# A second table of rank offsets for a list scheduler, by kind of work and by stretch of its plan

## The chip, the cores and the metric

The kernel runs on one core of a Trainium2 chip. The metric is device time in microseconds (us) of one execution; several executions are timed and their median is taken. TensorE is called PE below (PEld is its weight load), VectorE DVE, ScalarE ACT, GpSimd POOL, and SyncE SP; SP issues every DMA of this kernel.

## The reference, cut to what matters

Two attention layers read the same input `x` (2048 tokens, width 640, 32 heads of 20), and a gate per token mixes their outputs. Layer A works through four segments of 512 tokens, with a causal softmax inside the segment and a linear memory that is carried from one segment to the next; layer B is attention in a sliding window of 256.

```python
# layer A, segment s of 4 (H = 32 heads, Dh = 20)
logits = einsum("bhqd,bhkd->bhqk", qs, ks) * scale + mask
a_dot = einsum("bhqk,bhkd->bhqd", softmax(logits), vs)
num = einsum("bhld,bhde->bhle", phi(qs), M)
den = einsum("bhld,bhd->bhl", phi(qs), z)[..., None] + 1e-6
o = g * num / den + (1 - g) * a_dot
M = M + einsum("bhld,bhle->bhde", phi(ks), vs)
z = z + einsum("bhld->bhd", phi(ks))
...
# layer B
scores = where((i >= j) & (i - j < 256), q @ k.T * Dh ** -0.5, -1e9)
b = (softmax(scores) @ v) @ wo
...
return gate * a + (1 - gate) * b        # gate = sigmoid((x * gate_w).sum(-1))
```

## The kernel before, in words

All work is cut into 16 groups T: four segments of 512 tokens times four sets of 16 heads (two sets for A, two for B). A group holds four units of four heads, which makes 64 units u. The work of a group:

- **Projections.** `gemm2` (line 548) makes 128 rows of q and k for 512 tokens, `v_mm` (line 689) 128 tokens of v. Operands are float32 split into a high and a low part in float32r, three products each (`PAIRS`). Both use half of the array at a time: rows 0 to 63 or rows 64 to 127. Two such matmuls on different halves run side by side, so what counts is how long each half is kept fed. The output projection uses `gemm2` too.
- **Weights.** Each weight tile is loaded by SP (`load`, line 494, tile `wst`), its high part is copied by ACT (`split_h`, line 486), its low part is made by POOL or DVE (`split_l`, line 502), and only then may a matmul use it. There are two staging buffers `wst` and three weight buffers `w`. The weights of v go the same way from `wvs` (line 519), five pieces each; tokens go from `xst` to `xhl`.
- **Maxima.** Stacked q and k of a unit come back from DRAM into `qks` (lines 762 to 767). `max_mm` (line 791) makes scores in a bank, DVE takes their row maximum (`max_red`, line 801, a reduction and a read of the accumulator), and the maxima go through DRAM (`dmx`, lines 817 and 821) to become two more rows of `qks`. Each half of the array has one bank for this (`NMX` is 1), so that the next matmul of maxima on that half waits for the reduction of the last.
- **Scores and values.** `st_mm` (line 845) makes the transposed scores, ACT takes their exponential (line 852), POOL cuts the masked corners (lines 858, 861), and `tiled_mm` (line 877) multiplies with v. It uses 32 columns of the array at a time, as do the reads and sums of the memory (lines 904 and 924). DVE, POOL and ACT then normalise, and SP stores the output (line 993).

**What sets the order.** `Plan.add` records each piece of work with an engine, an assumed duration, a due time and what it reads and writes. `Plan.order` is a list scheduler: it steps through a planned time, asks on each engine which recorded pieces could start, keeps those that could start within 3 ns (PE, `TP`) or 25 ns (the others, `TO`) of the earliest, and takes the one with the lowest rank. The rank is the due time plus an offset from the table `SHIFT`, by kind of work (18 kinds) and by 18 stretches of four units of due time. The order in which pieces are taken is the order in which each engine gets its instructions; engines then run in that order and wait on semaphores. Where a piece may go to two engines (a split to POOL or DVE, a copy to ACT or DVE), the scheduler chooses too. So an offset that swaps two pieces changes the planned time from there on, and with it every later choice.

Of the kernel before, what the change touches and what calls it, by code (L numbers as in the profile page):

```python
# [39 lines left out]
TP, TO, GP = 0.003, 0.0247, -0.9848  # L40
# [16 lines left out]
KINDS = dict(v_mm="v", max_mm="x", st_mm="s", tiled_mm="t", mem_add="a", split_h="h", split_l="l", m_high="e", m_low="e", v_out="e",  # L57
             y_out="e", phi_neg="p", phi_exp="p", phi_sum="p", max_red="r", st_exp="c", select="k", load="d", wv_load="d",
             qk_store="q", stack_read="z")
SHIFT = dict(  # L60
    a=(0.906, 0.762, 0.711, 0.288, -0.209, -3.157, -0.759, -0.444, 2.687, -1.073, -0.036, -1.619, 0.786, -0.987, 0.501, -1.076, 1.313, -0.983),
    c=(0.731, -0.093, -0.385, -0.167, -0.708, 0.703, 0.113, -0.061, 0.619, -0.11, -1.531, 0.072, -0.295, 0.055, -0.214, 0.043, -0.116, 0.411),
    d=(0.746, 0.239, 0.185, -0.082, 0.39, -0.063, 0.049, 0.317, -0.528, -0.276, -0.057, 0.559, -0.263, -1.344, -0.501, -0.266, 0.361, 1.353),
    e=(-4.249, 1.705, -0.128, 1.795, -1.311, 0.375, 0.842, -0.859, -0.461, 0.272, 0.494, -0.544, -0.178, -0.287, 2.233, 0.044, -2.89, 1.8),
# [12 lines left out]
    y=(-0.053, 0.457, 3.475, -0.742, 3.085, 0.939, 0.479, 0.047, 0.088, -0.236, -0.012, 0.322, 0.417, -0.102, -0.234, -0.183, 1.517, -0.737),  # L77
    z=(-1.272, 0.109, 0.692, -0.168, -1.3, -1.064, -0.08, -0.22, 0.395, -0.261, 1.106, -0.382, 1.384, 1.123, 1.476, -0.094, 0, -0.095))


def f(ap):
    return ap.bitcast(F32)
# [9 lines left out]
class Plan:  # L92
# [37 lines left out]
    def clock(self, t, dur, cols):  # L130
# [8 lines left out]
            left -= part  # L139
        return at - t  # L140

    def shift(self, z):

        name = z[4].__name__
        kind = ("y" if z[5][0][0] == "y" else "m") if name in ("gemm", "gemm2") else KINDS.get(name, "o")
        return SHIFT[kind][min(max(int((z[0] + 6) // 4), 0), 17)] if SHIFT else 0.0

    def link(self):
        items = [(*z[:19], z[19] + self.shift(z)) for z in sorted(self.items, key=lambda z: z[:2])]
# [79 lines left out]
    def order(self):  # L229
        items, deps, succ, miss, trail, uses, left, kind = self.link()  # L230
        n = len(items)
        ready = [0.0] * n
        free, cand, dma = {}, {}, [0.0] * self.RINGS
        for e in ENGINES:
            cand[e] = set()
            if e != "pe":
                free[e] = 0.0
        on = [None] * n

        def offer(i):  # L240
            for e in items[i][2].split("|"):
                cand[e].add(i)
        for i in range(n):
            if not miss[i]:
                offer(i)
        out, self.starts, self.ticks = [], [], {}
        last, port = ("half", 1.0), 0.0
        lane, turns = [0.0] * LANES, 0
        half = ("pe0", "pe1")
        avail, held, until, self.bank = {b: 0.0 for b in range(self.BANKS)}, {}, {}, {}  # L250
        while len(out) < n:
            best, front = None, None
            both = max(free["pe0"], free["pe1"])
            for e in ENGINES:
                pe = e[:2] == "pe"
                begin = both if e == "pe" else free[e]
                cold = pe and self.cold(begin)
                some = []
                for i in cand[e]:
                    at = begin  # L260
                    if pe:
                        at += max(0.0, self.LOAD[items[i][13][0]] - last[1])
                    z = max(at, ready[i]) + (items[i][15] if last[1] > 0.06 else 0.0)
                    if items[i][16] and e in ("dve", "pool"):
                        z = max(z, port)
                    if items[i][14]:
                        b = items[i][14]
                        if len(avail) < len(b) or any(held.get(k, 0) >= most for k, most, _ in b):
                            continue
                        if b[0][0] == "pj" and sum(held.get(k, 0) for k in ("st0", "st1", "pj")) >= CAP:  # L270
                            continue
                        z = max(z, sorted(avail.values())[len(b) - 1])
                    if "|" in items[i][2]:
                        ways = items[i][2].split("|")
                        z += FT * (items[i][0] > FL or items[i][0] < FE) * (items[i][3][ways.index(e)] - min(items[i][3])) + (DP if e == "dve" else 0.0)
                    if e == "sp":
                        z = max(z, lane[turns % LANES])
                    if items[i][10] and items[i][10][0] > BULK:
                        z = max(z, max(dma[:items[i][10][1]]) - BACK)
                    if e == "pe" and z <= both + 0.12 and (front is None or items[i][19] < front[1]):  # L280
                        front = z, items[i][19]
                    if e in half and front and front[1] < items[i][19] and z + items[i][3] > front[0] + GP:
                        continue
                    some.append((z, cold and items[i][12] < 900, items[i][19], i))
                if some:
                    most = min(some)[0] + (TP if pe else TO)
                    pick = min((z for z in some if z[0] <= most), key=lambda z: z[1:])
                    if best is None or pick < best[0]:
                        best = (pick, e)
            (start, _, _, i), e = best  # L290
            if "|" in items[i][2]:
                ways = items[i][2].split("|")
                start -= FT * (items[i][0] > FL or items[i][0] < FE) * (items[i][3][ways.index(e)] - min(items[i][3])) + (DP if e == "dve" else 0.0)
            elif e[:2] == "pe" and last[1] > 0.06:
                start -= items[i][15]
            for k, _, name in items[i][14]:
                held[k] = held.get(k, 0) + 1
                b = min(avail, key=lambda b: (max(avail[b], start - 1.0), avail[b]))
                self.bank[name] = b
                del avail[b]  # L300
            many = items[i][2].split("|")
            for z in many:
                cand[z].discard(i)
            on[i] = e
            out.append(i)
            dur, size = items[i][3], items[i][10]
            if len(many) > 1:
                dur = dur[many.index(e)]
            if e[:2] == "pe":
                start = max(start, (both if e == "pe" or last[0] != items[i][13][0] else free[e]) + self.turn(last, items[i][13]))  # L310
                dur = self.clock(start, dur, items[i][12])
                if e == "pe" or last[0] != items[i][13][0]:
                    free["pe0"] = free["pe1"] = start + (dur if e == "pe" else 0.0)
                last = items[i][13]
                if e != "pe":
                    free[e] = start + dur
                e = "pe"
            else:
                free[e] = start + dur
            self.starts.append(start)  # L320
            if items[i][16] and e in ("dve", "pool"):
                port = start + dur
            if size:
                took, rings, late = size
                done = 0.0
                for k in range(rings):
                    dma[k] = max(dma[k], start + dur + 1.2) + took
                    done = max(done, dma[k])
                done += DM + late
                lane[turns % LANES] = done  # L330
                turns += 1
            else:
                done = start + dur
            for name in uses[i]:
                left[name] -= 1
                until[name] = max(until.get(name, 0.0), done + (0.0 if e == "pe" else self.TO_PE))
                if not left[name]:
                    avail[self.bank[name]] = until[name]
                    held[kind[name]] -= 1
            for j in trail[i]:  # L340
                ready[j] = max(ready[j], start)
                miss[j] -= 1
                if not miss[j]:
                    offer(j)
            for j in succ[i]:
                to = "pe" if items[j][2][:2] == "pe" else items[j][2]
                lag = ((0.0 if e == "pe" else XS) if to == e and not size else self.TO_PE if to == "pe" else
                       0.0 if size else self.FROM_PE if e == "pe" else self.OTHER)
                ready[j] = max(ready[j], done + lag)
                miss[j] -= 1  # L350
                if not miss[j]:
                    offer(j)
        self.span = max(free.values())
        return [(items[i][4], items[i][5] + ((on[i],) if "|" in items[i][2] else ()), items[i][0]) for i in out]
# [934 lines left out]
```

## Time and profile before

| | |
|---|---|
| three runs | 992.94, 995.86 and 1002.88 us; median 995.86 |
| the profiled execution | 1005.22 us |
| its span, first to last instruction | 1003.5 us; 1.72 us lie around it |
| instructions in the span | 30570, of them 11295 matmuls |
| mean granted clock of PE | 0.989 of full |
| moved by DMA | 248.57 MB, 248 GB/s over the span |

A row of the list by time reads: start in us, duration in us, engine, line, operation, what it writes and reads, how many are merged (x), and in brackets how long the engine was idle before it and what ended that. In the list by window, each engine has its busy time in that window and, in brackets, the number of its instructions; behind it stand the granted clock, the busy share of the DMA engines, and GB/s. In the chain of waits, a row is start, duration and the work that stood last in the way. A matmul's duration in the trace reaches to its modelled end, and two matmuls overlap; the distance from start to start is what PE spends on one.

### The profile page before, as it was taken

Reading aid. Unit: us, or ns where it says so; the run is one execution under the profiler, and the core shown is the slowest. Engines: PE = TensorE matmul, PEld = TensorE weight load, DVE = VectorE, ACT = ScalarE, POOL = GpSimd, SP = SyncE. Lnnn points to the kernel's source line nnn. Section 1 sums busy time; section 2 is a strip of 40 time slices with the busy share of each in tenths; the row PEclk is TensorE's granted clock in tenths of the full one; section 3 lists DMA queues with packets and bytes.
Section 4 is the critical chain, followed back from the end, with each engine's and each line's share of the span. In section 5 each row is a group of like instructions: output and inputs, shape, how many; then the busy total and the mean of one; then the engine's idle time right before and its main releaser. Section 6 shows DMA issues by size and latency. Waiting matters only on the chain.

```text
span 1003.5 us, 30570 instructions
## 1 busy us (share of the span) xinstructions
PE 984.1 (98%) x11295; PEld 826.2 (82%) x11295; DVE 759.3 (76%) x2638; ACT 666.9 (66%) x1601; POOL 634.5 (63%) x862
## 2 busy tenths in 40 slices
PE   8999999999999899999999999899999999999998
PEld 6998888788788688888988898778888888987776
DVE  3269788888789586887867887569777886788944
ACT  4447767878578575776867676575677766765672
POOL 4335565847665587766966478576686657955660
PEclk8999999999999999999999999899999999999999
DMA  8898888789887889878798787859977898486532
GB/s 271 277 301 270 279 273 286 235 272 283 256 251 234 275 232 281 267 257 278 247 279 269 232 267 220 262 168 307 296 242 228 247 302 278 144 260 204 182 97 100
DMA packets 158037, 248.57 MB, mean 248 GB/s; under 512 B 52032, under 2 KB 68288, under 8 KB 157888
## 3 DMA queue, kind: packets, MB, share of 16 engines
q1 hardware_dynamic: 157888, 246.62, 78.0%
q8 instruction: 89, 1.46, 0.6%
q14 instruction: 60, 0.49, 0.1%
HBM read 150.88 MB, written 95.68 MB: 246 GB/s over the span
## 4 chain that ended last, share of the span: by engine, by line
PE 86%; DMA 6%; DVE 4%; SPq 1%; ACT 1%; POOL 1%; issue 1%; DVEq 0%
PE bank L548 40%; PE bank L689 14%; PE bank L877 14%; PE bank L791 8%; PE bank L845 7%; DMA wst<-wqk 3%; DVE bank L801 2%; PE bank L540 1%; PE bank L904 1%; DMA dphi<-phi 1%; DMA wvs<-wv 1%; DMA qks<-dkb 1%; DMA qks<-dmx 1%; PE bank L924 1%; POOL w L502 0%
## 5 line engine op out<-in xcount | busy, mean ns | idle before, releaser
L852 ACT ACTIVATE P<-bank 128x512 f32<-128x512 f32 (+2 forms) x768 | 382.2, 552 | 113.4 <-PE bank L845 73.2
L548 PE MATMUL bank<-xhl,w 64*128 64x512 f32 x2400 | 456.1, 402 | 0.5 <-DVE xhl L502 0.5
L548 PEld LDWEIGHTS bank<-xhl,w 64*128 64x128 f32 x2400 | 328.8, 188 | 12.0 <-DVE xhl L502 1.5
L791 PE MATMUL bank<-qks 60*128 60x384 f32 (+3 forms) x1024 | 302.7, 336 | 4.9 <-DMA qks<-dkb 4.1
L689 PE MATMUL bank<-wv,xhl 64*128 64x320 f32 (+1 forms) x1920 | 292.8, 318 | 2.2 <-ACT wv L486 1.9
L801 DVE CUSTOM_DVE_ANT_0 bank<-bank,mask_b 128x384 f32<-128x384 f32 (+2 forms) x512 | 259.3, 554 | 30.2 <-PE bank L791 24.2
L801 DVE CUSTOM_DVE_ANT_0 bank<-bank,mask_a 128x256 f32<-128x256 f32 (+3 forms) x512 | 239.5, 511 | 44.6 <-PE bank L791 29.3
L845 PE MATMUL bank<-qks 62*128 62x384 f32 (+3 forms) x1216 | 264.6, 303 | 5.3 <-ACT P L852 3.3
L689 PEld LDWEIGHTS bank<-wv,xhl 64*128 64x128 f32 x1920 | 248.9, 189 | 6.7 <-ACT wv L486 2.3
L548 PE MATMUL bank<-ohl,w 64*128 64x512 f32 x1050 | 225.4, 399 | 1.4 <-ACT P L852 1.0
L502 POOL TENSOR_TENSOR w<-wst,w 128x640 fp32r<-128x640 f32 x109 | 170.3, 1565 | 86.3 <-ACT w L486 81.0
L858 POOL TENSOR_SCALAR_AFFINE_SELECT P<-P 128x512 f32<-128x512 f32 x256 | 161.5, 638 | 89.1 <-ACT P L852 71.3
L845 PEld LDWEIGHTS bank<-qks 62*128 62x128 f32 x1216 | 197.5, 186 | 23.2 <-ACT P L852 5.3
L791 PEld LDWEIGHTS bank<-qks 60*128 60x128 f32 x1024 | 177.2, 185 | 23.7 <-issue 11.3
L877 PE MATMUL bank<-P,vau 128*32 128x384 f32 (+3 forms) x2432 | 160.3, 408 | 0.4 <-DVE mx L801 0.2
L548 PEld LDWEIGHTS bank<-ohl,w 64*128 64x128 f32 x1050 | 153.6, 186 | 7.8 <-ACT P L852 1.5
L801 DVE DVE_READ_ACCUMULATOR2_ANT mx<- 128x1 f32 x1024 | 143.2, 140 | 0.0
L877 PEld LDWEIGHTS bank<-P,vau 128*32 128x32 f32 x2432 | 69.5, 110 | 78.7 <-issue 63.2
L486 ACT ACTIVATE w<-wst 128x640 fp32r<-128x640 f32 x121 | 89.1, 738 | 39.8 <-DMA wst<-wqk 24.4
L948 DVE STREAM_TRANSPOSE ot<-bank 128x512 f32<-128x512 f32 x64 | 45.8, 715 | 71.1 <-PE bank L877 68.2
L861 POOL TENSOR_SCALAR_AFFINE_SELECT P<-P 128x512 f32<-128x512 f32 x112 | 71.3, 645 | 8.8 <-ACT P L852 7.7
L502 POOL TENSOR_TENSOR wv<-wvs,wv 128x322 fp32r<-128x322 f32 x80 | 66.3, 845 | 12.1 <-ACT wv L486 11.7
(74 smaller groups left out, 790.9 us busy)
## 6 DMA issues: line engine op xcount, KB each, us to landing
qks<-dqk SPq DMA_DIRECT2D x32, 1024.0 KB
wst<-wqk SPq DMA_DIRECT2D x80, 320.0 KB
qks<-dkb SPq DMA_DIRECT2D x24, 768.0 KB
qks<-dqb SPq DMA_DIRECT2D x32, 512.0 KB
o_dram<-ot SPq DMA_DIRECT2D x64, 256.0 KB
wst<-wo SPq DMA_DIRECT2D x41, 320.0 KB
wvs<-wv SPq DMA_DIRECT2D x16, 805.0 KB
xst<-o_dram SPq DMA_DIRECT2D x35, 256.0 KB
```

The lines of the kernel that those rows point to most:

```text
L486: nc.scalar.activation(dst, src, AF.Copy)
L502: EN[e].tensor_tensor(out=t[:, 1], in0=B.pop(src), in1=f(t[:, 0]), op=ALU.subtract)
L548: nc.tensor.matmul(B[key], B[wkey][64 * r:64 * r + 64, a, 128 * c:128 * c + 128], B[xkey, c][64 * r:64 * r + 64, b], start=start, stop=sto ...
L689: nc.tensor.matmul(B["v", T, b][:, :n], B[("x", s), c][64 * r:64 * r + 64, a, 128 * b:128 * b + 128], B["wv", T, c][64 * r:64 * r + 64, bb ...
L791: nc.tensor.matmul(psum(("mx", u, p, b, r))[:, :n], fr(q), keys(u, 3 * DH, r, p, c0, n), start=True, stop=True)
L801: nc.vector.tensor_tensor_reduce(out=x, in0=x, in1=mk, scale=1.0, scalar=BIG, op0=ALU.add, op1=ALU.max, accum_out=B["M", u][:, j:j + 1])
L845: nc.tensor.matmul(B[k][:, c:c + 128 * n], keys(u, K, r, p, WIN + 128 * kb, 128), fr(q[64 * r:64 * r + K, L * p + 128 * q0:L * p + 128 * ( ...
L852: nc.scalar.activation(B["P", u, b][:, 2 * r + p, c0:c1], B["st", u, b, p, r][:, c0:c1], AF.Exp, scale=SCALE)
L858: nc.gpsimd.affine_select(out=v, in_=v, pattern=[[0, 4], [1, 128]], compare_op=ALU.is_ge, fill=0.0, base=0, channel_multiplier=-1)
L861: nc.gpsimd.affine_select(out=v, in_=v, pattern=[[0, 4], [-1, 128]], compare_op=ALU.is_gt, fill=0.0, base=0, channel_multiplier=1)
L877: nc.tensor.matmul(o[32 * j:32 * j + 32, 128 * q0:128 * (q0 + n)], v[:, VA * h:VA * h + 32], t[:, j, c:c + 128 * n], start=(b == 0 and i = ...
L948: nc.vector.transpose(t, B["o", u])
```

## The change

A second table, `NUDGE`, holds 151 offsets by kind of work and by stretch of 12.5 us of planned time. At each step the scheduler works out which stretch the planned time of PE lies in, and the rank of each candidate gets the offset of its kind for that stretch, on top of the offset from `SHIFT`. Kinds and stretches that are not listed get nothing. The recorded pieces, their engines to choose from, sizes, buffers and assumed durations are as before.

```diff
+STEP = 12.5
+NUDGE = dict(
+    a={22: 0.6},
+    c={12: 1, 39: 1.4, 47: 1.4, 51: -1.1, 53: 2.1, 74: 2.9},
...
+    v={1: -2.021, 3: -0.77, 5: -0.05, 9: 0.113, 17: -1.1, 25: -0.007, 34: -0.164, 39: -0.3, 45: -0.23, 49: 0.034,
+       52: -0.858, 65: -0.3, 68: -0.04, 69: -0.61},
...
     def order(self):
         items, deps, succ, miss, trail, uses, left, kind = self.link()
         n = len(items)
+        nudge = [NUDGE.get(self.kind(z), {}) for z in items]
...
             both = max(free["pe0"], free["pe1"])
+            step = int(both / STEP)
...
                 for i in cand[e]:
+                    rank = items[i][19] + nudge[i].get(step, 0.0)
...
-                    if e == "pe" and z <= both + 0.12 and (front is None or items[i][19] < front[1]):
-                        front = z, items[i][19]
-                    if e in half and front and front[1] < items[i][19] and z + items[i][3] > front[0] + GP:
+                    if e == "pe" and z <= both + 0.12 and (front is None or rank < front[1]):
+                        front = z, rank
+                    if e in half and front and front[1] < rank and z + items[i][3] > front[0] + GP:
                         continue
-                    some.append((z, cold and items[i][12] < 900, items[i][19], i))
+                    some.append((z, cold and items[i][12] < 900, rank, i))
```

The lines named below stand 30 further down in the changed kernel (548 becomes 578, and so on). The order changes from the first microseconds to the end. Four places follow.

**SP at the start of the program, before the change.** `wst` are tiles of weights, `xst` of tokens, `wvs` the first weights of v, and `dqk0` gets its rows of padding.

```order
L494 DMA xst_160<-xt 128x512
L494 DMA wst_175<-wqk 128x640
L412 DMA bet_87<-beta 128x1x8
L519 DMA wvs_180<-wv 128x5x322
L494 DMA xst_195<-xt 128x512
L494 DMA wst_206<-wqk 128x640
L455 DMA dqk0_108<-ot_158 128x128 x4
```

SP at the same place, with the change:

```order
L524 DMA xst_160<-xt 128x512
L442 DMA bet_87<-beta 128x1x8
L524 DMA wst_176<-wqk 128x640
L485 DMA dqk0_108<-ot_158 128x128 x4
L524 DMA xst_191<-xt 128x512
L524 DMA wst_206<-wqk 128x640
L549 DMA wvs_214<-wv 128x5x322
```

The weights of v move behind the padding, the fifth tile of tokens and the third tile of weights.

**PE in the same place, right behind the warm-up,** before the change (`xhl` are split tokens, `wv_239` and its like split pieces of the weights of v):

```order
L548 MATMUL bank<-xhl,w 128x512 x24
L689 MATMUL bank<-wv_239,xhl 128x322 x9
L689 MATMUL bank<-wv_241,xhl 128x322 x7
L689 MATMUL bank<-wv_244,xhl 128x322 x6
L689 MATMUL bank<-wv_254,xhl 128x322 x6
```

PE there with the change:

```order
L578 MATMUL bank<-xhl,w 128x512 x52
L719 MATMUL bank<-wv_269,xhl 128x322
L578 MATMUL bank<-xhl,w 128x512 x3
L719 MATMUL bank<-wv_269,xhl 128x322
L578 MATMUL bank<-xhl,w 128x512
```

The matmuls of v begin after 52 instead of 24 matmuls of q and k, and the first of them are spread among the others.

**PE behind the values of unit 0,** before the change (845 are scores of unit 1, 791 scores for maxima of unit 3, 548 is projection):

```order
L791 MATMUL bank<-qks_92 128x256
L845 MATMUL bank<-qks_90 128x512
L791 MATMUL bank<-qks_92 128x256
L791 MATMUL bank<-qks_92 128x384 x2
L845 MATMUL bank<-qks_90 128x512
L845 MATMUL bank<-qks_90 128x384
L845 MATMUL bank<-qks_90 128x128
L791 MATMUL bank<-qks_92 128x512
L845 MATMUL bank<-qks_90 128x384
L845 MATMUL bank<-qks_90 128x128
L791 MATMUL bank<-qks_92 128x512
L548 MATMUL bank<-xhl,w 128x512
```

PE there with the change:

```order
L907 MATMUL bank<-P,vau_93 32x256 x4
L875 MATMUL bank<-qks_90 128x512 x2
L821 MATMUL bank<-qks_92 128x384 x2
L875 MATMUL bank<-qks_90 128x512 x2
L821 MATMUL bank<-qks_92 128x512
L875 MATMUL bank<-qks_90 128x384
L821 MATMUL bank<-qks_92 128x512
L875 MATMUL bank<-qks_90 128x128
L875 MATMUL bank<-qks_90 128x384
L578 MATMUL bank<-xhl,w 128x512
```

Of the seven matmuls for maxima that stood ahead of the first projection, three (one of 128 columns, which stands ahead of the rows shown, and two of 256) have moved ahead of the values.

**SP where the weights of group 2 are loaded,** before the change (`qks` are stacked q and k, `pks` rows for the memory):

```order
L594 DMA dqb_110<-ml 96x2x512
L592 DMA dqb_110<-ml 96x512
L494 DMA wst<-wqk 128x640
L594 DMA dqb_110<-ml 64x2x512
L592 DMA dqb_110<-ml 64x512
L594 DMA dkb_112<-ml 64x2x512
L592 DMA dkb_112<-ml 64x512
L885 DMA pks<-dphi_114 20x32x32 x2
L494 DMA wst<-wqk 128x640
```

SP there with the change:

```order
L622 DMA dqb_110<-ml 96x512
L792 DMA qks_90<-dqk_108 128x2x1024
L915 DMA pks<-dphi_114 20x32x32 x4
L624 DMA dqb_110<-ml 64x2x512
L792 DMA qks_91<-dqk_108 128x2x1024
L622 DMA dqb_110<-ml 64x512
L624 DMA dkb_112<-ml 64x2x512
L622 DMA dkb_112<-ml 64x512
L847 DMA dmx<-mt 4x32x32
L524 DMA wst<-wqk 128x640 x2
```

The two weight tiles of the second pair of projections of group 2, which were issued apart, are issued one behind the other, after two stacks and four loads of `pks`.

More of the change, by code (lines that the diff above doesn't have):

```diff
@@ L78 @@
     z=(-1.272, 0.109, 0.692, -0.168, -1.3, -1.064, -0.08, -0.22, 0.395, -0.261, 1.106, -0.382, 1.384, 1.123, 1.476, -0.094, 0, -0.095))
+STEP = 12.5
+NUDGE = dict(
+    a={22: 0.6},
+    c={12: 1, 39: 1.4, 47: 1.4, 51: -1.1, 53: 2.1, 74: 2.9},
+    d={8: 1.1, 15: -0.1, 22: -0.2, 24: -1.1, 25: 0.1, 27: 1.1, 38: -0.8, 42: -0.3, 43: -1.6, 44: -2.2},
+    e={13: -1.2, 17: 0.1, 30: 0.5, 34: 0.1, 39: -1.1, 41: -0.7, 42: 1.7, 44: -0.5, 54: -0.4, 58: 6.1, 66: -0.1},
+    h={19: 2.7, 22: 0.4, 31: -1.8, 33: 0.5, 37: 2.8, 46: -2, 60: 0.4, 61: -0.1, 66: -0.4},
+    k={10: -0.3, 36: 1.5, 57: 2.4, 61: -0.5},
+    l={50: -1.4, 61: -0.3},
+    m={1: -0.289, 3: 0.18, 5: -0.215, 10: 0.89, 18: 0.24, 19: 0.45, 29: -0.26, 35: -0.024, 40: -0.357, 42: 0.75,
+       52: 0.31, 56: -0.15, 57: 0.71, 59: -0.58, 64: -0.01, 66: -0.1},
+    o={0: -1.6, 2: 2.8, 4: -1.2, 13: -0.9, 14: 0.3, 23: 0.01, 25: -0.6, 26: 1, 35: 0.02, 37: 2, 40: 1, 41: 1.4,
+       44: -1.3, 46: -0.04, 52: -1, 53: 1.1, 67: -0.4, 69: -0.9},
+    p={14: -1.4, 15: -1.13, 51: -1.5},
+    q={23: -0.021, 25: 0.7, 37: 2.6, 43: 0.4, 66: -0.1},
+    r={26: 1.2, 37: 1.2, 38: -0.8, 66: 1.3, 68: 1.6},
+    s={15: 0.03, 17: -0.08, 19: 0.02, 20: -0.2, 24: 2.1, 40: 0.03, 45: 0.3, 51: -0.26, 53: 0.378, 54: 0.15,
+       61: -0.03, 67: -0.02, 68: 0.67, 69: -0.01, 71: 0.3, 72: 0.13},
+    t={11: -0.01, 59: -0.02},
+    v={1: -2.021, 3: -0.77, 5: -0.05, 9: 0.113, 17: -1.1, 25: -0.007, 34: -0.164, 39: -0.3, 45: -0.23, 49: 0.034,
+       52: -0.858, 65: -0.3, 68: -0.04, 69: -0.61},
+    x={9: 0.7, 16: 0.1, 26: -0.3, 37: -0.8, 53: 0.49, 55: 1.1, 58: -0.009, 62: 0.1, 64: 0.13, 72: -0.02},
+    y={20: -0.9, 24: -0.1, 25: -0.396, 26: -0.51, 29: -0.52, 33: -0.1, 43: -0.2, 45: -0.014, 48: 0.12, 52: -0.01,
+       53: 0.4, 61: 0.14, 63: 0.8},
+    z={4: 1.4, 7: -1.7, 23: -0.9, 50: 5.2, 55: 1.4, 59: -2})
 def f(ap):
@@ L140, in clock, with kind @@
         return at - t
+    def kind(self, z):
+        name = z[4].__name__
+        return ("y" if z[5][0][0] == "y" else "m") if name in ("gemm", "gemm2") else KINDS.get(name, "o")
     def shift(self, z):
-        name = z[4].__name__
-        kind = ("y" if z[5][0][0] == "y" else "m") if name in ("gemm", "gemm2") else KINDS.get(name, "o")
-        return SHIFT[kind][min(max(int((z[0] + 6) // 4), 0), 17)] if SHIFT else 0.0
+        return SHIFT[self.kind(z)][min(max(int((z[0] + 6) // 4), 0), 17)] if SHIFT else 0.0
     def link(self):
```

## The prediction, on record before the result

> **What bounds the kernel now.** I read the page first: how busy each engine is, and the chain of work that ended last.
>
> ```profile
> span 1003.5 us, 30570 instructions
> PE 984.1 (98%) x11295; PEld 826.2 (82%) x11295; DVE 759.3 (76%) x2638; ACT 666.9 (66%) x1601; POOL 634.5 (63%) x862
> PE 86%; DMA 6%; DVE 4%; SPq 1%; ACT 1%; POOL 1%; issue 1%; DVEq 0%
> ```
>
> PE has work in flight for 984.1 of 1003.5 us, and 86% of the chain is PE. An order can win only what PE stands idle, 19.4 us, and what it does badly while it counts as busy: it counts as busy when one half of the array works and the other is empty. The list by window says where the idle time is.
>
> ```profile
> 0.00:20.00 20.00, 16.49 (x95) 12.23 (x97) 7.57 (x14) 9.28 (x18) 9.00 (x22) 0.83 0.79 244
> 60.00:100.00 40.00, 39.21 (x418) 34.40 (x418) 37.26 (x146) 22.56 (x56) 14.68 (x19) 0.97 0.88 280
> 260.00:340.00 80.00, 74.07 (x905) 59.74 (x903) 59.24 (x208) 50.92 (x126) 43.86 (x61) 0.98 0.84 260
> 610.00:650.00 40.00, 36.67 (x452) 31.52 (x451) 27.00 (x100) 25.55 (x57) 30.91 (x41) 0.96 0.76 220
> 650.00:920.00 270.00, 270.00 (x3141) 226.33 (x3138) 211.18 (x733) 183.48 (x442) 184.18 (x246) 0.99 0.77 246
> 982.00:1003.50 21.50, 17.68 (x77) 14.01 (x76) 9.79 (x13) 4.50 (x7) 1.51 (x2) 0.97 0.34 116
> ```
>
> 3.5 us at the start, 3.8 at the end, 0.8 between 60 and 100, where DVE is busy 37.26 of 40, and 9.3 in two stretches, 260 to 340 and 610 to 650; nothing in 270 us from 650 on. The two stretches are transfers that came late: the chain of waits has in them
>
> ```profile
> 260.76 8.11 DMA wst<-wqk
> 329.01 7.33 DMA qks<-dkb
> 638.68 8.57 DMA wst<-wqk
> ```
>
> The Trainium skill (Perfetto Trace Analysis, Identifying the Most-Contended Engine) would not take matmul busy time as the measure, since matmuls are pipelined, but the busy share of weight loads. By that the room here is 177 us (82% of 1003.5 used), by the idle time 19.4. The first is no bound an order can reach, since half the matmuls overlap the other half; it agrees that 98% hides something, and the half-empty array below is it.
>
> **The change part by part.** The same instructions run, so nothing is added or removed; I price four moves.
>
> *The start.* In the first 25 us, the lists by time of PE and of POOL, the chain of waits, the list of SP, and windows of lines 548 and 689 alone:
>
> ```profile
> 6.02 2.28 PE L548 MATMUL bank<-xhl,w 64*128 64x512 f32 x14
> 9.88 0.73 PE L548 MATMUL bank<-xhl,w 64*128 64x512 f32 x4 [0.23 <-DVE xhl L502]
> 13.48 4.39 PE L689 MATMUL bank<-wv,xhl 64*128 64x322 f32 x26 [0.33 <-POOL wv L502]
> 19.94 3.58 PE L548 MATMUL bank<-xhl,w 64*128 64x512 f32 x29
> 23.29 1.21 PE L689 MATMUL bank<-wv,xhl 64*128 64x322 f32 x13
> 24.26 0.39 PE L548 MATMUL bank<-xhl,w 64*128 64x512 f32 x1
> ```
>
> ```profile
> 12.55 5.00 POOL L502 TENSOR_TENSOR wv<-wvs,wv 128x322 fp32r<-128x322 f32 x5 [7.82 <-ACT wv L486]
> ```
>
> ```profile
> 4.37 7.60 DMA wvs<-wv
> ```
>
> ```profile
> 4.37 0.42 SPq L519 DMA_DIRECT2D wvs<-wv  x1
> 7.23 2.67 SPq L455 DMA_DIRECT2D dqk<-ot  x4
> ```
>
> ```profile
> 0.00:21.90 21.90, 8.32 (x48) 0.84 0.81 255
> 0.00:21.90 21.90, 6.90 (x37) 0.84 0.81 255
> ```
>
> Undisturbed, 29 projections take 3.58 us; less the tail of the last (0.39) that is 0.114 us each, 0.228 per half. For v it is (1.21 - 0.31) / 12 = 0.075. The last two rows are lines 548 and 689 up to 21.9 us: 48 and 37 matmuls, worth 48 x 0.114 + 37 x 0.075 = 8.25 us. From 10.6 to 13.5 PE waits for the first weights of v, with two matmuls in between, and then goes at the pace of POOL, which splits their five pieces in 5.00 us. With the change SP issues `wvs` behind the padding (2.67 us) and two more loads, at about 8.7 instead of 4.4 us. With the same 7.60 us it lands at 16.3, and POOL is done at 21.9. But in the new order 68 projections and 21 matmuls of v stand ahead of the first that needs the fifth piece, 68 x 0.114 + 21 x 0.075 = 9.3 us of work, and no piece of v holds up the first 52. So at 21.9 PE has done 9.3 us instead of 8.25: a gain of 1.1. With less traffic ahead of it the load may land 2 us sooner, and PE is not held to 21.9: 3.1. I take **-2.1**; the ends are +0.5 (it lands 1.6 us later) and -3.3. Up to the first maxima both orders hold nearly the same PE work (300 and 297 projections), so DVE's busy stretch begins earlier by what is gained.
>
> *The hole behind unit 0.* PE by time around 94 us, DVE in the chain of waits, and one window:
>
> ```profile
> 93.71 0.51 PE L845 MATMUL bank<-qks 62*128 62x512 f32 x2
> 94.80 0.49 PE L845 MATMUL bank<-qks 62*128 62x512 f32 x1 [0.47 <-DVE ot L948]
> 96.01 0.78 PE L845 MATMUL bank<-qks 62*128 62x512 f32 x2 [0.15 <-DVE mx L801]
> 97.33 0.54 PE L548 MATMUL bank<-xhl,w 64*128 64x512 f32 x1
> ```
>
> ```profile
> 92.29 0.19 DVE bank L801
> 94.98 0.32 DVE bank L801
> 95.31 0.06 DVE mx L801
> ```
>
> ```profile
> 95.00:100.00 5.00, 4.85 (x27) 4.04 (x28) 4.96 (x17) 4.33 (x10) 4.31 (x5) 0.76 1.00 352
> ```
>
> From 93.71 to 97.33, 3.6 us, PE has only scores. By their columns (0.228 per 512 and half) they are worth 1.2 us, so 2.4 are lost, mostly as a half-empty array, while they wait for DVE one by one. In the new order three of the seven maxima (128 and two of 256 columns) stand ahead of the values; on DVE they are 0.19 + 0.06 and twice 0.32 + 0.06. I take **-1.0**, between 0 and -2.4.
>
> *Balance of the halves.* Between two blocks of 32-column work (line 877 and its like) the array drains, so in each such stretch the longer half counts. I added up columns per half, from the order and the row group of each matmul: the longer halves come to 702.4 us before and 700.2 with the change, that is -2.2. One more block is cut off (the sums of the memory of unit 0 stand alone), 65 instead of 64.
>
> ```profile
> 286.70 0.39 PE L548 MATMUL bank<-xhl,w 64*128 64x512 f32 x1
> 287.02 2.36 PE L877 MATMUL bank<-P,vau 128*32 128x512 f32 x32
> ```
>
> ```profile
> PEld bank L877 <- issue: 63.2, 277, 0.7
> ```
>
> From the last projection to the block is 0.32 us where 0.23 is usual; waits of this kind of weight load come to 63.2 / 64 = 1.0 per block, though off PE's own row. One more block costs 0.1 to 1.0; I take 0.5. Together **-1.7**; the ends are 0 (the empty half was waiting for something anyway) and -2.1. The rule in the Trainium skill (TensorEngine Tiling, Key Properties) that a change of tiling mode drains the engine speaks against this edit in that one block alone, and the trace agrees to 0.1 us on entry.
>
> *Weights with less cover.* The way of a late weight tile:
>
> ```profile
> 89.28 1.05 SPq L494 DMA_DIRECT2D wst<-wqk  x2
> 93.97 0.74 ACT L486 ACTIVATE w<-wst 128x640 fp32r<-128x640 f32 x1
> 94.78 1.55 POOL L502 TENSOR_TENSOR w<-wst,w 128x640 fp32r<-128x640 f32 x1 [1.36 <-ACT w L486]
> ```
>
> Issue to split is 96.33 - 89.28 = 7.05 us. I counted how much PE work the orders leave between a load of `wst` and its first matmul. Behind the first 10 us of work, the thinnest covers were 5.5, 8.0, 8.9 and 9.5 us, and five more up to 10.7; now they are 4.7, 6.0, 7.1, 7.2, 7.7, 8.2 and 8.7, and four more up to 10.0. The 4.7 is the pair that SP now issues behind two stacks and four `pks`; POOL and PE queue behind it in order. What 7.05 lacks was 1.55 and is 2.35 + 1.05 = 3.4: **+1.9**. Below, it is 0 where the load lands early; above, with the 8.57 us of the row at 638.68 plus the splits (10.9 in all) for every load, it is +16.6.
>
> Stacks (`qks`) have as much cover as before (4.3 and 4.1 at the thinnest, a quarter below 9.2 and 8.7). In the last 80 us the orders leave DVE and PE the same work behind each unit's values, so they get nothing. The waits at 329 and 638 may move but I have no reason for fewer.
>
> Sum: -2.1 - 1.0 - 1.7 + 1.9 = **-2.9**. The profiled execution took 1005.22 us; with the change it would take 1002.3. It lies 9.4 us above the median of the runs shown, 995.86, about as much as the idle time of the two late stretches, so runs may differ by such transfers. For the median: 995.86 - 2.9 = **993.0 us**.
>
> **The rivals.** *The late transfers go.* The idle 5.9 us in 260 to 340 and 3.3 in 610 to 650 hang on three loads; in another order they meet other traffic. For it: 270 us from 650 on have none, so they are not built in. Against it: DMA is as busy as before and covers are no thicker. Without them 9.3 us more: 983.7.
>
> *No gain at all.* DVE is busy 37.26 of 40 us from 60 to 100; if it, not PE, sets the pace until unit 4, what the start and the balance win there is waited away, and the late weights cost what the rest gains: 995.9, the median of before. For it: DVE's rows in the fence on the hole stand back to back. Against it: three maxima leave DVE's way just there.
>
> *Weights come late.* One mechanism: the loads with thin cover stall PE, and the clock falls behind each hole; at 95 us it was 0.76 for 5 us, worth 1.2. It decides from the point where issue to split takes over 8.5 us: then the lack grows from 3.5 to 10.1, and the extra 6.6 exceed the other terms' 4.8. At 10.9 us it is 16.6 plus five holes at 1.2, less the balance: +20.9 with the start at 0, 1016.8. Halfway it is 1006. For it: 8.11 and 8.57 us of landing stand in the chain, and at 60 to 65 us, where the 4.7 lies, loads are dense. Against it: with short covers before, nothing stalled longer than this from 650 on.
>
> **How the numbers follow.** The forecast 0.42; the late transfers go, 0.25; no gain, 0.18; late weights, 0.15. A measurement of this kernel can tell about 1% from no change (three runs span 992.94 to 1002.88), that is below 985.9 and above 1005.8. Faster by over 1%: the first rival and a little of the forecast, 0.28. Slower by over 1%: late weights beyond halfway, 0.12. Within: 0.60. The forecast's own ends: all gains full and no late weights give -7.8 (988.1); no gains and weights as priced give +2.4 (998.3). The range reaches from 982, a little beyond the first rival, to 1003, part of the way into the last.
>
> **What would show it.** Right: projections fill PE from about 13 to 17 us, with more than 55 of line 578 by 21.9 us; the first maxima on DVE come about 2 us before 61; the hole behind unit 0 lasts under 3 us; PE is busy over 98%. Wrong: PE waits for `wv` later but as long; a wait for weights near 70 us that is not there now; idle time elsewhere of more than 9 us, or the stretch from 650 on no longer without holes.

## The result, and the profile after

The change takes **985.23 us** in the median (983.94 to 987.68, six runs), against 997.92 (992.94 to 1002.88, six runs) for the kernel before, timed beside it: a ratio of 0.9873 (95% interval 0.9836 to 0.991), so 12.7 us or 1.3% faster. The forecast was 2.9 us and 993.0. The profiled execution took 985.39 us; it lies at its own median, while that of before lay 7.3 above the median of these six runs.

The page of the change, the line of busy times and the chain that ended last (as shown of before):

```profile
span 983.7 us, 30582 instructions
PE 973.6 (99%) x11295; PEld 816.6 (83%) x11295; DVE 763.6 (78%) x2648; ACT 663.5 (67%) x1589; POOL 637.2 (65%) x864
PE 89%; DMA 5%; DVE 3%; SPq 1%; issue 1%; ACT 1%; POOL 0%; ACTq 0%; DVEq 0%
```

The span is 19.8 us shorter. Idle time of PE gives 9.3 of that (19.4 to 10.1); the other 10.5 us come out of its *busy* time, with the same 11295 matmuls. So something in "busy" got better: a half of the array stands empty less often, or the clock is higher. By an estimate from these two executions the clock is about half of it: it was granted at 0.995 on the mean instead of 0.989, and 0.006 of 984 us is 5.9.

The change by window:

```profile
0.00:20.00 20.00, 16.52 (x91) 11.28 (x93) 5.62 (x11) 8.99 (x18) 9.50 (x23) 0.83 0.88 279
60.00:100.00 40.00, 38.70 (x403) 32.92 (x402) 36.58 (x141) 23.39 (x56) 17.83 (x21) 0.96 0.84 254
260.00:340.00 80.00, 79.95 (x974) 66.31 (x973) 69.99 (x245) 58.64 (x146) 50.91 (x68) 1.00 0.88 276
610.00:650.00 40.00, 40.00 (x569) 33.29 (x569) 30.44 (x108) 26.81 (x65) 26.51 (x37) 1.00 0.91 282
963.00:983.70 20.70, 16.86 (x75) 13.57 (x73) 9.76 (x13) 3.71 (x6) 2.14 (x2) 1.00 0.35 120
```

The idle 5.9 and 3.3 us of the two late stretches are gone (0.05 and 0). The stretch from 60 to 100 is worse (1.3 us idle instead of 0.8). The start and the end are as idle as they were. Transfers are as slow as they were; the chain of the change still has

```profile
69.34 7.38 DMA dkb<-ml
332.71 8.11 DMA wst<-wqk
585.12 8.31 DMA qks<-dqk
```

but only the first is followed by a hole in PE (0.59 and 0.28 us, shown further down); behind the third PE waits 0.2 us, behind the second it has no wait. ACT's waits for weight tiles, before and then after:

```profile
ACT w L486 <- DMA wst<-wqk: 24.4, 17, 4.0
```

```profile
ACT w L516 <- DMA wst<-wqk: 9.2, 11, 1.5
```

So weights with "less cover" are waited for less, not more. The traces of the experiments agree: 6.3 to 10.3 us in the three kernels that have the changed order over most of the run, 10.5 to 20.4 in the others (without `queue_new`).

### The profile page after: what moved, and what is told of

It reads as the page before. It is cut to its first block, busy times and chain, and to the rows that moved or that the text cites. A ratio compares the mean times of both kernels' runs of the same rounds, so it can differ in the third digit from the quotient of the medians.

```text
span 983.7 us, 30582 instructions
## 1 busy us (share of the span) xinstructions
PE 973.6 (99%) x11295; PEld 816.6 (83%) x11295; DVE 763.6 (78%) x2648; ACT 663.5 (67%) x1589; POOL 637.2 (65%) x864
## 4 chain that ended last, share of the span: by engine, by line
PE 89%; DMA 5%; DVE 3%; SPq 1%; issue 1%; ACT 1%; POOL 0%; ACTq 0%; DVEq 0%
PE bank L578 41%; PE bank L907 15%; PE bank L719 13%; PE bank L821 8%; PE bank L875 8%; DVE bank L831 2%; DMA wst<-wqk 2%; PE bank L570 2%; PE bank L934 1%; DMA qks<-dqk 1%; DMA o_dram<-ot 1%; DMA dkb<-ml 1%; PE bank L954 1%; DMA xst<-xt 0%; DMA dqk<-ml 0%
## 5 line engine op out<-in xcount | busy, mean ns | idle before, releaser
L821 PE MATMUL bank<-qks 60*128 60x384 f32 (+3 forms) x1024 | 310.7, 335 | 1.2 <-DVE ml L592 0.6
L719 PE MATMUL bank<-wv,xhl 64*128 64x320 f32 (+1 forms) x1920 | 281.1, 313 | 0.2 <-ACT tick_act L516 0.2
L831 DVE CUSTOM_DVE_ANT_0 bank<-bank,mask_a 128x128 f32<-128x128 f32 (+3 forms) x512 | 240.4, 511 | 39.6 <-PE bank L821 28.4
L875 PE MATMUL bank<-qks 62*128 62x384 f32 (+3 forms) x1216 | 259.9, 301 | 0.5 <-DVE ot L978 0.2
L719 PEld LDWEIGHTS bank<-wv,xhl 64*128 64x128 f32 x1920 | 239.2, 186 | 3.7 <-issue 1.2
L532 POOL TENSOR_TENSOR w<-wst,w 128x640 fp32r<-128x640 f32 x112 | 174.9, 1565 | 79.3 <-ACT w L516 54.6
L888 POOL TENSOR_SCALAR_AFFINE_SELECT P<-P 128x512 f32<-128x512 f32 x256 | 161.6, 640 | 77.8 <-ACT P L882 66.1
L907 PEld LDWEIGHTS bank<-P,vau 128*32 128x32 f32 x2432 | 69.4, 110 | 78.5 <-issue 63.2
L592 DVE TENSOR_TENSOR ml<-bank,ml 128x512 fp32r<-128x512 f32 x80 | 53.7, 682 | 25.6 <-ACT ml L588 20.2
```

Of the source, the lines that this page charges most:

```text
L532: EN[e].tensor_tensor(out=t[:, 1], in0=B.pop(src), in1=f(t[:, 0]), op=ALU.subtract)
L592: nc.vector.tensor_tensor(out=t[:, 1], in0=B[k], in1=f(t[:, 0]), op=ALU.subtract)
L719: nc.tensor.matmul(B["v", T, b][:, :n], B[("x", s), c][64 * r:64 * r + 64, a, 128 * b:128 * b + 128], B["wv", T, c][64 * r:64 * r + 64, bb ...
L821: nc.tensor.matmul(psum(("mx", u, p, b, r))[:, :n], fr(q), keys(u, 3 * DH, r, p, c0, n), start=True, stop=True)
L831: nc.vector.tensor_tensor_reduce(out=x, in0=x, in1=mk, scale=1.0, scalar=BIG, op0=ALU.add, op1=ALU.max, accum_out=B["M", u][:, j:j + 1])
L875: nc.tensor.matmul(B[k][:, c:c + 128 * n], keys(u, K, r, p, WIN + 128 * kb, 128), fr(q[64 * r:64 * r + K, L * p + 128 * q0:L * p + 128 * ( ...
```

## The experiments

At a few places the two orders have done nearly the same work, so that one can be continued by the other. The scheduler is run twice, without and with the table, and the two lists of 12,719 steps are joined. All these kernels carry the change's line numbers.

```diff
-    def order(self):
+    def order(self, NUDGE):
...
-        for fn, a, _ in self.order():
+        for fn, a in spliced(self):
             fn(*a)
...
+    old, w0, b0 = plan.order({})
+    new, w1, b1 = plan.order(NUDGE)
```

At the cuts used for the table further down, the sets of PE steps done in the two orders differ by at most seven, so times from cut to cut can be compared between any two traces.

### Four parts, each alone

```diff
+    for part, w in ((old[:lo], w0), (new[:hi], w1), (old, w0)):
+        for i in part:
+            if i not in seen:
+                seen.add(i)
+                seq.append(i)
+                way[i] = w[i]
+    seq, plan.bank = banked(plan, seq)
```

with lo and hi at 0 and 1,100; 1,100 and 5,470; 5,470 and 8,700; 8,700 and the end. `banked` gives each new tile of PE's results the bank (of eight) that was freed first.

> All engines take the changed order for the first 1,100 of the 12,719 steps (both traces reach that point at about 96 us) and the old order from there on, so the start, the ramp of the first units and the hole behind unit 0 are those of the change. Late loads (my theory now: the gain comes from loads that stood too far back on SP's queue in the middle of the run): no gain, -0.5 to +0.5 us, since the two traces reach this point at 96.0 and 96.5 us. The terms of the prediction: the start and the hole give -3.1 us. Chance (the waits seen in the trace of before are those of one bad execution, and the gain is spread over the whole run like PE's work): a tenth of 12.7 us, -1.3.

> The changed order from step 1,100 to step 5,470 alone (96 to 424 us in the trace of before, 96 to 413 in that of the change); here lie the waits at 260 and 329 us. Late loads: this part carries the larger half of the gain; the traces differ by 11.2 us here, of which the profiled execution of before, 7.3 us above its median, may have overstated a part: -6 to -9 us. The terms of the prediction: -1.4 us of balance and +1.9 us of weights with less cover, +0.5. Chance: a third of 12.7, -4.

> The changed order from step 5,470 to step 8,700 alone (424 to 670 us before); here lie the waits at 638 us. Late loads: the traces differ by 7.9 us here: -4 to -6 us. The terms of the prediction: 0 (the longer halves are 0.2 us longer here). Chance: a quarter of 12.7, -3.

> The changed order from step 8,700 to the end alone (the last 333 us, in which the trace of before has no idle time up to 982). Late loads: -1 us, which is the balance of the halves (1.0 us shorter here), and the traces differ by 1.2. The terms of the prediction: also -1. Chance: a third of 12.7, -4.

Ratios to before: part 1 1.0001 (0.9978 to 1.0025), part 2 1.0011 (0.9987 to 1.0035), part 3 1.0003 (0.9982 to 1.0024), part 4 1.0082 (1.0052 to 1.0112). No part gains, and the last loses some 8 us. All theories fail as they stood: four parts of a gain of 12.7 add up to a loss. Two differences from the change itself were left: the seams, where one order hands over to the other, and the banks. In the old order, first freed first given puts 255 of 2,113 tiles behind another tile than the scheduler planned.

### The same parts with the planned banks, one load moved, and SP's order alone

For parts 2 and 4, each piece carries the banks of its own plan (and the first cut lies at 1,145); part 4 is the same with 8,700 and the end:

```diff
+    for part, w, b in ((old[:1145], w0, b0), (new[:5470], w1, b1), (old, w0, b0)):
...
+        pieces.append((part, b))
+    seq, plan.bank = banked(plan, seq, pieces)
```

One load moved (`stack22_early`; 4191 and 4192 are the loads of the stacks of unit 22, 4111 a store):

```diff
...
+    for what, ahead in [([4191, 4192], 4111)]:
+        queue = [i for i in queue if i not in what]
+        queue[queue.index(ahead):queue.index(ahead)] = what
+    seq = merge(plan, way, [i for i in seq if way[i] != "sp"], queue)
```

SP's order alone (`queue_new`):

```diff
+    rest, way, plan.bank = old, w0, b0
+    queue = [i for i in new if way[i] == "sp"]
+    seq = merge(plan, way, [i for i in rest if way[i] != "sp"], queue)
```

> The old order and its banks, but SP issues the two loads of the stacks of unit 22 eleven places earlier, ahead of eight stores of queries and keys, two loads of maxima and one store of phi (which each come two places later). Everything else is the old order. Late load: steps 3,900 to 4,300 took 37.4 us in the trace of before and 34.6, 35.0 and 35.3 in the three kernels that have the old order there, but 29.2 and 29.3 in the two that have the changed one; this alone gives -4 to -6 us in the median and about 30 us in that stretch. Rival, the wait only moves (the stores then land later, and the next load or unit 23 is late instead): 0, and the next two stretches are longer by what this one is shorter.

> The changed order from step 1,145 to step 5,470, as in the earlier kernel of this part (which began at 1,100 and gave no gain), but each PSUM tile gets the bank that its own order planned; the earlier kernels gave the bank that was freed first, which puts some 255 of 2,113 tiles behind another tile. Banks (the other banks cost the four earlier kernels 4 to 5 us each and hid the gain): -6 to -9 us. Whole (the gain does not divide: each order fits only with its own rest): 0 again. Late load of unit 22 alone: -5.

> The changed order from step 8,700 on, with the banks that the orders planned; the earlier kernel of this part was 7 us slower than before, of which its trace has 4 to 5 in one wait for the stacks behind the cut (steps 8,700 to 9,200: 43.4 us against 38.2 to 39.7). Banks: -1 to +1 us, and the wait behind the cut is gone. Whole: +7 again, with the wait at the cut, since the cut sets a late load of one order ahead of the early use of the other.

> The old order and banks on PE, DVE, ACT and POOL; SP alone takes its queue in the changed order, save 20 of 1,034 items that had to go earlier because the old order of the others needs them first. Late loads (it is SP's order that makes the gain): -6 to -10 us, and the runs spread less, like those of the change (4 us from lowest to highest instead of 10). Whole: a queue that does not fit the others' order makes new late loads: +2 to +10 us. The terms of the prediction: 0, since the start moves by SP alone but the balance stays.

**Part 2 with planned banks** gains: 0.9955 (0.9929 to 0.9982), that is 4.5 us, where the same part with other banks had 1.0011 with an interval that does not touch this one. What differs is the bank of the tiles (and 45 steps at the first cut), so here the banks are very likely part of what the order is worth, some 5 us. It is one pair of kernels: the same comparison of parts 3 and 4, below, gives 1.4 and 2.2 us, with intervals that overlap; part 1, which has the old order with other banks from step 1,100 on, lost nothing; and the whole old order with other banks was not run. The gain is less than the 6 to 9 us expected.

**The one load** gives nothing: 0.9999 (0.9976 to 1.0022). The move did what it should. SP and windows of before, then of this kernel:

```profile
329.01 1.05 SPq L765 DMA_DIRECT2D qks<-dkb  x1
...
320.00:340.00 20.00, 15.94 (x162) 13.13 (x161) 9.06 (x33) 9.61 (x24) 11.33 (x15) 0.91 0.86 274
```

```profile
317.61 0.42 SPq L795 DMA_DIRECT2D qks<-dkb  x1
...
320.00:340.00 20.00, 19.12 (x208) 16.07 (x207) 13.04 (x45) 13.39 (x33) 14.14 (x18) 1.00 0.88 282
```

The load goes out 11.4 us earlier, PE is busy for 3.2 us more of these 20, and the clock is 1.00 instead of 0.91: some 5 us in this one pair of traces. Yet the median stays. So the longest wait in the profile of before was mostly that execution's own: over steps 3,891 to 4,748, around it, that execution took 68.3 us, the same order in two other kernels with planned banks 63.2 and 66.2, in three with other banks 64.2 to 65.9, and this kernel 64.2.

**Part 4** loses again, 1.006 (1.0031 to 1.0089), and again at the seam. The chain of waits of this kernel, PE's waits from 665 to 720 us, and the windows there:

```profile
666.11 7.28 DMA qks<-dkb
```

```profile
PE bank L821 <- DMA qks<-dkb: 3.3, 1, 3.3
```

```profile
665.00:673.50 8.50, 4.86 (x89) 2.08 (x82) 4.08 (x14) 3.77 (x10) 6.42 (x8) 0.93 0.83 245
673.50:681.00 7.50, 7.47 (x48) 7.50 (x49) 4.07 (x14) 4.92 (x11) 3.81 (x6) 0.63 0.67 187
```

A stack load that the two orders place differently comes late; PE waits 3.3 us for it, and then works for 7.5 us at a clock of 0.63, which costs 2.8 us more (0.37 x 7.5). Steps 8,706 to 10,107 take 110.0 us instead of 103.6 to 104.6: the seam is 6 us. Banks did not cure it; the expectation "whole" was right here.

**SP's order alone** is far slower: 1231.85 us, ratio 1.2365 (1.2316 to 1.2414), clock 0.912. PE's waits:

```profile
PE bank L875 <- DMA qks<-dmx: 62.7, 17, 7.0
PE bank L821 <- DMA qks<-dqk: 26.5, 7, 8.6
PE bank L821 <- ACT P L882: 17.8, 6, 7.1
```

That SP's order carries the gain by itself falls with it. PE's longest waits are for stacks and maxima, which fits a queue in which an item that stands ahead of what the others have ready holds up all behind it; no wait of SP was followed up here. SP's order can't be changed without the others'; the reverse, the other four orders with SP's old one, was not run.

### Three combinations, and part 3

```diff
+    for part, w, b in ((old[:1145], w0, b0), (new, w1, b1)):                            # no_start
+    for part, w, b in ((new[:635], w1, b1), (old[:1145], w0, b0), (new, w1, b1)):       # no_hole
+    for part, w, b in ((new[:8706], w1, b1), (old, w0, b0)):                            # no_tail
+    for part, w, b in ((old[:5470], w0, b0), (new[:8700], w1, b1), (old, w0, b0)):      # part3_b
```

> The old order up to step 1,145 and the changed one from there on, with planned banks. Sum of stages (the gain is the sum of many small pieces; eight traces put the changed order 2.2 us ahead at step 635 and 2.2 us back again between 635 and 1,098): the start nets nothing, so all of the change's gain is here, -12 to -13 us against before. The terms of the prediction: 3.1 us less than the whole change, -9 to -10.

> The changed order up to step 635, the old one from 635 to 1,145 (the ramp of the first units and the hole behind unit 0), the changed one from 1,145 on, with planned banks. If the start's 2.2 us and the 2.2 us that are lost behind it belong to two pieces of order, both are to be had: -15 us against before, which beats the change, and steps 635 to 1,098 take about 35.0 us as in the old order. Rival (what the start wins is waited away before step 1,098, since DVE or the clock sets the pace of the ramp, as the prediction's rival of no gain says): those steps take 37 us again and the whole is -12.7.

> The changed order up to step 8,706 and the old one from there on, with planned banks: the counterpart of the last part, which alone made the kernel 6 us slower through a wait for the stacks at its seam. Sum of stages (behind 8,706 the changed order is 0.7, 0.9 and 0.95 us shorter in three stages): -10 us. Late loads alone: -12.7, since no wait for a load lies behind 8,706. Whole (a seam costs some 6 us wherever it lies): -4.

> The changed order from step 5,470 to step 8,700 alone, with planned banks; with the banks that were freed first it gave nothing (+0.0, -0.2 to +0.2 per cent), though its trace has 66.8 us for steps 7,797 to 8,706, where seven executions of the old order have 66.7 to 74.0 (mean 69.4). Sum of stages: -3 us, and a smaller spread than before's, since the old order has a late load there in about three of seven executions. Whole: 0.

Ratios: `no_start` 0.9927 (0.9901 to 0.9952), -7.3 us; `no_hole` 0.994 (0.9915 to 0.9965), -6.0; `no_tail` 0.9928 (0.9899 to 0.9957), -7.2; part 3 (`part3_b`) 0.9989 (0.9963 to 1.0014), -1.1 and not to be told from nothing. None beats the change. `no_hole` misses its 15 us by far: steps 635 to 1,098 take 38.6 us with the old order behind the new start, no less than with the new order.

### What the traces say from cut to cut

From the nine traces of kernels with planned banks, each entry the time between the starts of PE's last step before either cut; the mean and, in brackets, lowest and highest, with the number of traces. Left out are the stretches right behind a seam of part 4 and `no_tail`, the second stretch of `no_hole`, and that around the moved load.

| steps | old order | changed order | difference |
|---|---|---|---|
| 0 to 635 | 61.1 (59.6 to 62.4), 6 | 58.9 (58.7 to 59.1), 3 | -2.2 |
| 635 to 1,098 | 34.9 (34.2 to 36.5), 6 | 38.0 (37.5 to 38.5), 2 | +3.1 |
| 1,098 to 3,891 | 201.6 (199.7 to 203.5), 4 | 199.3 (197.9 to 200.2), 5 | -2.3 |
| 3,891 to 4,748 | 65.9 (63.2 to 68.3), 3 | 63.5 (62.5 to 64.2), 5 | -2.5 |
| 4,748 to 5,464 | 56.2 (56.0 to 56.3), 4 | 55.5 (55.4 to 55.5), 5 | -0.7 |
| 5,464 to 7,797 | 173.2, 4 | 173.0, 5 | -0.2 |
| 7,797 to 8,706 | 71.1 (67.4 to 74.0), 4 | 67.2 (66.1 to 69.9), 5 | -4.0 |
| 8,706 to 10,107 | 104.1 (103.6 to 104.6), 4 | 103.6 (103.1 to 104.0), 3 | -0.5 |
| 10,107 to 11,097 | 73.3 (72.6 to 73.7), 5 | 73.2 (73.0 to 73.3), 4 | -0.1 |
| 11,097 to 12,161 | 85.8 (85.6 to 86.1), 5 | 84.7 (84.4 to 85.0), 4 | -1.1 |
| 12,161 to 12,523 | 31.5 (31.3 to 32.2), 5 | 30.7 (30.7 to 30.7), 4 | -0.8 |
| rest | 39.9, 5 | 39.8, 4 | 0.0 |

The differences add up to -11.2 us, inside what was measured for the whole (-9.0 to -16.4). So in these traces the gain is spread: up to step 1,098 the change loses 0.9, from there to 8,706 it gives 9.7, and behind that 2.5. The sum leans on the one trace of before, an execution 7.3 us above its median: without it the differences come to about -9. Two measured kernels also fall short of the table: `no_start` should have -12.1 by it and has -7.3 (-4.8 to -9.9), and part 3 (`part3_b`) should have -4.2 and has -1.1 (-3.7 to +1.4). The largest entry is also the least sure: in the old order that stretch took 67.4, 69.3, 73.8 and 74.0 us, and 66.7 to 67.3 in the three kernels of the first set that have the old order there with other banks. It is a place where the old order waits in some executions and not in others.

That fits the clock. Beside the experiments the kernel before was timed 85 times. Leaving out the two longest (1006.94 and 1007.91 us), it took 996.9 us in the mean, 989.5 to 1003.84, at a mean granted clock of 0.9936; over these 83, a clock that is lower by 0.001 goes with 1.04 us more (correlation -0.75). The change's six runs have 985.7 us at 0.9965. So 3.0 of 11.2 us go with the clock, which falls behind holes (0.63 behind the seam of part 4, 0.91 in before around the wait for unit 22); the rest is there at equal clock.

## Why the prediction was right or wrong

The direction was right and the size was not: -2.9 us were forecast and -12.7 measured. The range, 982 to 1003, holds the result only because it was stretched past the first rival; the forecast's own ends, 988.1 and 998.3, do not, so that is luck and not mechanism. "Faster by over 1%" had a chance of 0.28.

**The start, -2.1: right, and then lost.** The window of line 578 alone in the change, up to 21.9 us:

```profile
0.00:21.90 21.90, 13.10 (x68) 8.67 (x68) 0.84 0.81 257
```

The same of line 719, the matmuls of v:

```profile
0.00:21.90 21.90, 2.98 (x20) 2.76 (x22) 0.84 0.81 257
```

SP's issue of the weights of v, and behind it POOL's five splits of them:

```profile
7.84 0.43 SPq L549 DMA_DIRECT2D wvs<-wv  x1
```

```profile
15.64 3.97 POOL L532 TENSOR_TENSOR wv<-wvs,wv 128x322 fp32r<-128x322 f32 x5 [4.71 <-ACT wv L516]
```

68 and 20 matmuls are worth 68 x 0.114 + 20 x 0.075 = 9.25 us by the rates of the prediction, which said 9.3; POOL is done at 19.6, sooner than the 21.9 assumed. The first maxima come at 58.74 instead of 61.1. By step 635 the changed order is 2.2 us ahead. By step 1,098 the lead is gone. What takes it in the change begins on SP's queue:

```profile
59.55 6.90 SPq L915 DMA_DIRECT2D pks<-dphi  x4
...
69.34 0.77 SPq L622 DMA_DIRECT2D dkb<-ml  x1
```

It goes on in the list of ACT's waits from 64 to 98 us, and in DVE's list by time:

```profile
ACT ml L588 <- DMA dkb<-ml: 2.5, 1, 2.5
```

```profile
77.46 0.69 DVE L592 TENSOR_TENSOR ml<-bank,ml 128x512 fp32r<-128x512 f32 x1 [0.67 <-ACT ml L588]
```

PE's list by time at that place, and three windows of it:

```profile
76.78 0.46 PE L954 MATMUL bank<-pkn,vau 128*32 128x32 f32 x32
77.17 0.44 PE L821 MATMUL bank<-qks 60*128 60x256 f32 x2
78.20 1.35 PE L821 MATMUL bank<-qks 60*128 60x384 f32 x4 [0.59 <-DVE ml L592]
79.84 1.22 PE L578 MATMUL bank<-xhl,w 64*128 64x512 f32 x2 [0.28 <-DVE mx L831]
```

```profile
76.70:80.00 3.30, 2.43 (x40) 1.45 (x39) 2.63 (x12) 2.17 (x4) 1.84 (x3) 1.00 1.02 400
80.00:83.50 3.50, 3.50 (x16) 2.78 (x17) 2.61 (x14) 0.00 (x0) 1.42 (x1) 0.54 0.68 252
83.50:86.00 2.50, 2.50 (x25) 2.42 (x23) 2.46 (x10) 1.09 (x4) 0.00 (x0) 0.97 0.70 164
```

Four loads of `pks` hold SP for 6.9 us, 4.84 of them in a single load; the low part of a piece of q and k, ready at 63.5, is stored only from 66.6 to 70.1, and the last of these stores takes 7.38 us to land. Until then the buffer `ml` is not free; ACT waits, DVE behind ACT, and PE behind DVE. In before, the last store of the same piece goes out at 68.49, hardly sooner, yet ACT writes the next piece at 72.72 instead of 76.83. From 76.7 to 80.0 PE is idle for only 0.87 us and has small matmuls of the memory and maxima; then the clock is 0.54 for 3.5 us, worth 1.6 (0.46 x 3.5). This is the place that the order of SP in the section on the change shows last; I priced its two weight loads there (4.7 us of cover) and not the stores that were queued behind the `pks`. It is argued from the trace, and the kernel that would move the four loads behind the stores was not run. The `pks` can't be all of it: with the old order behind the new start (`no_hole`) the same 38.6 us were spent, and no load of `pks` up to 100 us took over 1.51 there. ACT waited as long for the landing of another store of keys, which took 6.38 us; from its list of waits from 60 to 100 us:

```profile
ACT ml L588 <- DMA dkb<-ml: 2.4, 1, 2.4
```

So what the two kernels share is a store of keys that lands late; why it does is open. The rival "no gain at all" had this right, that what the start wins is waited away on the ramp, though not by DVE alone.

The Trainium skill (TensorE: Matmul & The Clock Gate, Why this matters for your kernels) warns of idle gaps of more than about 3 us as what lowers the clock. This trace does not keep to that: no gap of such length stands before the fall, only 0.87 us of idle time in 3.3, the longest piece 0.59.

**The hole behind unit 0, -1.0: right.** PE in the change:

```profile
95.60 0.50 PE L875 MATMUL bank<-qks 62*128 62x512 f32 x2
...
98.17 0.50 PE L578 MATMUL bank<-xhl,w 64*128 64x512 f32 x1
```

2.6 us instead of 3.6. But the same stretch lost more at 77 us.

**Balance of the halves, -1.7: right in sign, in places.** Behind step 11,097, where PE waits 0.8 us in the trace of before and 0.2 in that of the change, the last three stretches give -1.9 us, in every trace alike (the second of them 30.7 us in four against 31.3 to 32.2 in five). The longer halves fall by 0.6 us there, so the term that the prediction priced is at most a third of it; what else was won, no run here tells.

**Weights with less cover, +1.9: wrong.** ACT's waits for weights fell from 24.4 to 9.2 us, and no wait for weights stands near 70 us. The step of this term that failed is the count of cover itself. It takes the distance in PE work from a load's place in the order to its first use, and assumes that SP is at that place when PE is. In before, SP was not: from 308.6 to 334.8 us its issues stand back to back, and from 320 to 340 us its items went out, in the mean, 3.2 us after PE had passed their place in the order; in the change it was 1.4 us before. The stack of unit 22 had 7.0 us of cover by the order (PE passed its place at 325.3 us and was at its first use at 332.4) and a landing of 7.33, which should cost 0.3. SP issued it at 329.01, 3.7 us late, and it cost 4.1:

```profile
336.43 0.58 PE L791 MATMUL bank<-qks 60*128 60x384 f32 x2 [4.07 <-DMA qks<-dkb]
```

**What was missing: "The waits at 329 and 638 may move but I have no reason for fewer."** This is the sentence that cost the forecast its size. The stretches with these two waits give -2.5 and -4.0 in the table, and the stretch before them -2.3; the rival "the late transfers go" named the kind of gain and with 983.7 came within 2 us of the result, at a chance of 0.25. It was right for half a reason. It priced the waits by the one profile, 9.3 us, and the one load that I moved shows that such a wait in a profile is not its mean: removed, it left the median as it was. The trace of the change has fewer such waits, and its six runs spread over 3.7 us where the six of before spread over 10. So the step that failed in the size is this one, at a price of nothing for want of a reason; what the runs showed in its place is the 6.5 us of these two stretches in the table, of which the profiled execution itself makes up a part. What in the order removes the waits they do not show.

Not settled: which pair of steps makes the old order's waits in the middle, since neither one load nor SP's order alone carries the gain; and why `no_start` has 7.3 us and the change 12.7 when the changed start loses 0.9 in the traces. Their intervals (-4.8 to -9.9 and -9.0 to -16.4 us) just overlap, and part of it is the kernel before, whose median was 997.92 beside the change and 995.74 beside `no_start`; the medians of the two kernels themselves, 985.23 and 987.59, lie 2.4 us apart.

## What to carry to other kernels

A wait in one profile is one execution's: before pricing its removal, compare the profiled time with the median and, if there are more traces, the same stretch in them. The order of five engines and the banks of its tiles are one object; a piece of it transplanted can cost at its seam (6 us here) half of what the whole had won, so predict such a change from how often PE is held up at all, and not from a sum over the edits seen. Where cover is counted in one engine's work, check first that the issuing queue keeps pace with that engine.

## What was not expected of the hardware

- The bank that a tile gets seems to matter by itself: the same part with planned banks and with those that were freed first, 0.9955 and 1.0011. One pair shows it; in two others the intervals overlap.
- The granted clock fell to 0.54 for 3.5 us behind 0.87 us of idle time, and to 0.63 for 7.5 us behind a wait of 3.3 us. At these two places the clock cost 1.6 and 2.8 us beyond the idle time itself.
- A run of four small loads held SP's queue for 6.9 us, 4.84 of it in one load, where the store quoted behind it took 0.77. In the two other kernels with the same four in a row (`part1`, `no_tail`) the longest took 5.00 and 4.05; in before, none of the eight such loads up to 100 us took over 2.64.
